# Moving a weight cast out of the down product's queue, and one gate into another PSUM bank, in an attention and bilinear-GLU kernel

## The chip, the cores and the metric

The kernel runs on one core of a Trainium2 chip. The metric is the device time of one execution in microseconds (us); differences under about 0.2% (4.6 us) cannot be told from no change. A profile is one execution: its rows give start times in us from the start of the span. PE is TensorE (PEld its weight loads), DVE is VectorE, ACT ScalarE, POOL GpSimd, and SP issues the DMAs.

## The reference

One pre-norm transformer layer on 2048 rows of 576 numbers, all in fp32: attention with 32 query heads of 18 and one shared key and value head, then a bilinear gated feed-forward part of width 4608 without a nonlinearity.

```python
def _A_ref(x, wq, wk, wv, wo):          # x: 1 x 2048 x 576, H = 32, Dh = 18
    q = (x @ wq).reshape(B, S, H, Dh).transpose(0, 2, 1, 3)
    k = x @ wk
    v = x @ wv
    scores = jnp.einsum("bhqd,bkd->bhqk", q, k) * (Dh ** -0.5)
    p = _softmax(scores, axis=-1)
    o = jnp.einsum("bhqk,bkd->bhqd", p, v)
    return o.transpose(0, 2, 1, 3).reshape(B, S, H * Dh) @ wo

def _B_ref(x, w_gate, w_up, w_down):
    g = jnp.einsum("bsd,df->bsf", x, w_gate)
    u = jnp.einsum("bsd,df->bsf", x, w_up)
    return jnp.einsum("bsf,fd->bsd", g * u, w_down)

h = x + _A_ref(_layernorm(x), wq, wk, wv, wo)
h2 = h + _B_ref(_layernorm(h), w_gate, w_up, w_down)
```

## The kernel before

The 2048 rows are worked on in four blocks of 512 (`NB`, `TB`). Each large fp32 product is made of three products of a rounded high part and a low part: a number is split into `hi` (a cast to the type fp32r) and `lo = x - f32(hi)`. The helper `split` issues both, the cast on an engine of the caller's choice (line L96 of the profile) and the subtraction on VectorE (L97).

The feed-forward part of blocks 0 to 2 is `ffn(b)`. It loops over 36 tiles of 128 hidden columns; tile `n_` is 36 b + f. For a tile TensorE runs 27 slots `j` (nine chunks of the input by three hi/lo combinations), in each slot one matmul for the gate (`pg`) and one for the up half (`pu`), line L1069. ScalarE copies the gate to `hf` (L1101), VectorE multiplies it by the up half (L1105). Two tiles make a pair; the down product of a pair (`down`, L1019) is issued at the end of the next even tile. It consists of 14 stages of three matmuls each (a seven-product scheme for 2 x 2 blocks), written out in the table `STAGES`, over three PSUM banks. After each stage the bank is added into the residual `h`: directly on VectorE (L1025, stages 0, 1, 3, 7, 9, 10, 12, 13), or by a copy to `tmp` on ScalarE (L1029) and an add on GpSimd (L1030; stages 2, 4, 5, 6, 8, 11). `tmp` has three buffers. Stages 9, 10, 12 and 13 begin a new sum in the banks of stages 6, 7, 9 and 10. The input of the down product is a split of `hf` and of sums `S` of its halves (`left`, `left_sums`, written to `room`).

Tiles are of two kinds. While attention work is left (`on`), its score matmuls and exponentials (L701, L702) and its value products (`acc`, L706) are laced into the gate/up slots; this holds for tiles 0 to 92. The last 15 tiles, 93 to 107, have none left and are called plain here. In plain tiles gate and up share the tile `gu` in PSUM, in the others each has a bank of its own: `ps_f` gives one of two banks in turn, `ps_m` and `ps_a` one each. `ps_a` is also the bank of the attention accumulator. At the end of an even tile the accumulator is closed (`flush(..., True)`): its last value products are issued, and VectorE saves it to `ob` (L719 or L748).

The order of the work on each engine is the order in which the code issues it (the schedule is manual); every engine works through its own queue, and so does the DMA queue of SP. The weights of a tile come in three steps: `load_w(n)` issues a DMA of 576 KB into `wr` (one buffer), and `split_w(n)` casts it on GpSimd into `ws` (two buffers) and subtracts on VectorE. The load of the next weights is issued behind the subtraction that frees `wr`. In plain tiles the split of the next tile's weights is issued at slot 9 of odd tiles, and in even tiles inside the down product, behind its stage 5.

When block 2 ends, block 3 is prepared on the side (`ahead`) and computed by `last_block` with another scheme (L1291 are its first matmuls). In tile 100 GpSimd runs the small chain of the reciprocal root for block 3's layer norm (L117 to L127).

Of the kernel before, what the change touches and what calls it, by code (L numbers as in the profile page):

```python
# [19 lines left out]
F32R = mybir.dt.float32r  # L20
I32 = mybir.dt.int32
AF = mybir.ActivationFunctionType
ALU = mybir.AluOpType
# [3 lines left out]
P = 128  # L27
# [30 lines left out]
class Block:  # L58
# [881 lines left out]
            r = self.wr[n] = self.wp.tile([P, 9, P], F32, tag="wr", bufs=1, name=f"wr{n}")  # L940
            self.sp.dma_start(r, self.wgu[n % NF])

    def split_w(self, n):
        if n < NF * (NB - 1):
            r = self.wr.pop(n)
            w = self.ws[n] = self.wp.tile([P, 2, 9, P], F32R, tag="ws", bufs=2, name=f"ws{n}")
            self.split(w[:, 0], w[:, 1], r, self.nc.gpsimd.tensor_copy)

    def load_wd(self, n):

# [91 lines left out]
    def ffn(self, b):  # L1042
        pe, act, dve = self.pe, self.act, self.dve
        X, hid, todo = self.X, [], None
        ahead = self.ahead()
        if b == 0:
            self.sums = self.weight_sums()
            next(self.sums)
        for f in range(NF):
            n_ = NF * b + f  # L1050
            k = f % 2
            w = self.ws.pop(n_)
            on = self.more(b + 2)
            self.cast_left = self.nc.gpsimd.tensor_copy if on else act.copy
            last = f == NF - 1 and b + 1 < NB
            end = b == NB - 2
            if on:
                pg = (self.ps_a if k and f > 1 and not last else self.ps_f)(f"pg{n_}")
                pu = (self.ps_f if k else self.ps_m)(f"pu{n_}")
            else:  # L1060
                gu = self.ps_s(f"gu{n_}")
                pg, pu = gu[:, 0], gu[:, 1]
            j = 0
            for c in range(9):
                for wk, xk in ((0, 0), (0, 1), (1, 0)):
                    if on and j in (PAIRS[2] if last else PAIRS[k]) and self.more(b + 2):
                        self.pair()
                    for o, ps in ((0, pg), (64, pu)):
                        pe.matmul(ps, w[o:o + 64, wk, c], X[o:o + 64, xk, c], start=(j == 0), stop=(j == 26))  # L1069
                    if j == (8 if on else 2) and todo and not plain(n_ - 2):  # L1070
                        self.left_sums()
                    if j == (3 if on else 9 if k else 27):
                        self.split_w(n_ + 1)
                    if j == (14 if on else 9 if k else 27):
                        self.load_w(n_ + 2)
                    if j == 5 and k:
                        self.left_first(n_ - 1, hid[0])
                    if j == 6 and not k:
                        self.split_wo()
                    if j == 12:  # L1080
                        self.run_aux(within=True, wo=False)
                    if 0 < f < NF - 1 and j in (8, 16, 24) and self.sums:
                        if next(self.sums, "end") == "end":
                            self.sums = None
                            self.load_wd(self.n_wd + 2)
                    if j == 6 and last and not end:
                        self.normal(b + 1)
                    if end and f == TURN - 1 and j == 12:
                        self.normed[NB - 1] = self.mv, self.rstd(self.mv[:, :, 1], "bl", self.nc.gpsimd)
                    if end and f in AHEAD and j in AHEAD[f]:  # L1090
                        for _ in range(AHEAD[f][j]):
                            next(ahead)
                    j += 1
            if todo and not on:
                for i, _ in enumerate(self.down(b, *todo)):
                    if i == 5:
                        self.split_w(n_ + 1)
                        self.load_w(n_ + 2)
                self.load_wd(self.n_wd + 7)
            hf = self.hh.tile([P, TB], F32, tag="hf", bufs=2, name=f"hf{n_}")  # L1100
            act.copy(hf, pg)  # L1101
            for _ in range(2 if on and not k else 0):
                if self.more(b + 2):
                    self.pair()
            dve.tensor_tensor(hf, pu, hf, ALU.mult)  # L1105
            hid.append(hf)
            if k:
                self.left(n_ - 1, hid)
                hid = []
            if end and f in TURNS:  # L1110
                for _ in range(TURNS[f]):
                    next(ahead)
            if not k or last:
                self.flush(len(self.pend), True)
            if todo and on:
                drain(self.down(b, *todo))
                self.load_wd(self.n_wd + 7)
            if f < NF - 1:
                self.run_aux(wo=k)
            todo = (f // 2,) if k else None  # L1120
        if end:
            del X, pg, pu, gu, w, ps, hf, self.X
            self.last_block(ahead, self.down(b, *todo))
            return
        both(self.spread(b + 1), self.down(b, *todo))
        self.load_wd(self.n_wd + 4)
        if b + 2 < NB:
            self.load_x(b + 2)
# [524 lines left out]
def both(a, b):  # L1653

    live = [a, b]
    while live:
        live = [x for x in live if next(x, drain) is not drain]


def plain(n):  # L1660

    return n % NF == NF - 2
# [6 lines left out]
def f32(ap):  # L1669
    return ap.bitcast(F32)  # L1670
# [20 lines left out]
def drain(gen):  # L1691
    for _ in gen:
        pass
# [85 lines left out]
```

## Time and profile before

| | us |
|---|---|
| median of 3 runs | 2297.33 (2295.97 to 2300.37) |
| profiled execution | 2295.53 |
| its span | 2293.7 |
| the plain tiles, 93 to 107, within it | 1785.5 to 1966.5 |
| VectorE's weight subtraction (L97), mean of 108 | 1.774 |
| GpSimd's weight cast (L96), mean of 108 | 1.193 |
| GpSimd's add into h (L1030), mean of 306 | 0.806 |

A row of a timeline names start, length, engine, line, operation, the tile written and the tiles read, shapes, a count (neighbouring instructions of one kind are merged) and, in brackets, how long the engine had been idle before and what ended that. A chain of waits is followed from the last instruction back: each piece is what the next one had to wait for.

### The profile page before, as it was taken

What the parts mean: (1) busy time and instruction counts of PE and PEld (TensorE: products, weight loads), DVE (VectorE), ACT (ScalarE), POOL (GpSimd) and SP (SyncE); (2) the same over time, 40 slices, a digit from 0 to 9 for tenths busy, and PEclk for the clock granted to TensorE, in tenths of its full rate; (3) what the DMA queues carried; (4) which work ended last, traced back from release to release, by engine and by line L of the source; (5) the groups of instructions that cost most, each with busy time, mean ns of one, the idle gap of its engine ahead of it and who ended that gap; (6) DMA issues with size and microseconds to landing.
All of it is one profiled execution on the core that took longest, in us unless ns stands there. A gap on an engine that the chain in (4) does not pass through costs nothing.

```text
span 2293.7 us, 45953 instructions
## 1 busy us (share of the span) xinstructions
PE 2239.2 (98%) x17972; PEld 1650.8 (72%) x17972; DVE 1380.1 (60%) x2234; ACT 1426.3 (62%) x1925; POOL 871.0 (38%) x956
## 2 busy tenths in 40 slices
PE   7999999999999999999999999999999888999999
PEld 5333345777777777777777787777777777899999
DVE  8555645555555566456555566545455666778876
ACT  7888877666666665666666666566666223555553
POOL 4445301444443444344443444342333342322222
PEclk9999999999999999999999999999999999999999
DMA  5879843555555554655554555653333344577775
GB/s 174 265 255 304 267 146 107 156 163 175 170 164 155 168 169 152 220 161 166 157 169 151 168 162 167 193 164 109 123 126 117 121 158 148 181 249 242 231 249 177
DMA packets 200433, 407.01 MB, mean 177 GB/s; under 512 B 22637, under 2 KB 54509, under 8 KB 200213
## 3 DMA queue, kind: packets, MB, share of 16 engines
q1 hardware_dynamic: 197621, 393.42, 53.8%
q0 software_dynamic: 2592, 10.62, 1.5%
q8 instruction: 143, 2.34, 0.4%
q14 instruction: 77, 0.63, 0.1%
HBM read 317.27 MB, written 74.55 MB: 171 GB/s over the span
## 4 chain that ended last, share of the span: by engine, by line
PE 82%; POOL 1%; DVE 1%; ACT 1%; DMA 1%; issue 1%; SPq 0%; ACTq 0%; POOLq 0%; DVEq 0%
PE pg L1069 16%; PE acc L706 15%; PE y L1019 12%; PE pu L1069 8%; PE s L701 8%; PE gs L1291 8%; PE gu L1069 4%; PE yq L1256 4%; PE yo L864 3%; PE gs L1298 1%; PE y L989 1%; POOL h L1030 1%; DVE ws L97 1%; ACT P L702 0%; DMA h<-in_x_dram 0%
## 5 line engine op out<-in xcount | busy, mean ns | idle before, releaser
L702 ACT ACTIVATE P<-s 128x1024 f32<-128x1024 f32 x1024 | 1009.9, 1028 | 222.7 <-PE s L701 141.6
L1069 PE MATMUL pg<-X,ws 64*128 64x512 f32 x2511 | 681.5, 389 | 4.5 <-ACT hf L1101 4.5
L1069 PE MATMUL pu<-X,ws 64*128 64x512 f32 x2511 | 681.2, 389 | 0.2
L1069 PEld LDWEIGHTS pg<-X,ws 64*128 64x128 f32 x2511 | 464.8, 185 | 60.2 <-issue 6.9
L1069 PEld LDWEIGHTS pu<-X,ws 64*128 64x128 f32 x2511 | 464.1, 185 | 25.7 <-ACT tmp L996 0.9
L706 PE MATMUL acc<-P,V 128*32 128x512 f32 x4096 | 480.0, 597 | 0.1
L701 PE MATMUL s<-q,kT 56*128 56x512 f32 x2048 | 430.9, 414 | 4.6 <-ACT P L702 3.5
L1030 POOL TENSOR_TENSOR h<-h,tmp 128x288 f32<-128x288 f32 x306 | 238.8, 806 | 406.2 <-ACT tmp L1029 391.4
L1029 ACT COPY tmp<-y 128x288 f32<-128x288 f32 x306 | 122.1, 399 | 380.5 <-PE y L1019 353.8
L1019 PEld LDWEIGHTS y<-wdo,room 128*128 128x128 f32 x2142 | 294.5, 191 | 67.5 <-issue 37.7
L1019 PE MATMUL y<-wdo,room 128*128 128x288 f32 x2142 | 309.8, 303 | 25.4 <-DVE h L1025 25.4
L701 PEld LDWEIGHTS s<-q,kT 56*128 56x128 f32 x2048 | 204.6, 184 | 167.2 <-ACT P L702 116.3
L706 PEld LDWEIGHTS acc<-P,V 128*32 128x32 f32 x4096 | 114.6, 109 | 255.1 <-issue 250.2
L97 DVE TENSOR_TENSOR ws<-wr,ws 128x1152 fp32r<-128x1152 f32 x108 | 191.6, 1774 | 119.3 <-POOL ws L96 117.8
L1025 DVE TENSOR_TENSOR h<-h,y 128x288 f32<-128x288 f32 x408 | 175.2, 452 | 121.0 <-PE y L1019 120.9
L1105 DVE TENSOR_TENSOR hf<-pu,hf 128x512 f32<-128x512 f32 x93 | 63.7, 685 | 224.9 <-ACT hf L1101 224.9
L96 POOL CAST room<-hf 128x256 fp32r<-128x256 f32 (+1 forms) x92 | 58.1, 632 | 320.1 <-DVE hf L1105 320.1
L96 POOL CAST ws<-wr 128x1152 fp32r<-128x1152 f32 x108 | 128.9, 1193 | 120.6 <-DMA wr<-in_wgu_dram 103.0
L1239 POOL TENSOR_TENSOR wsum<-wsum,wsum 128x512 f32<-128x512 f32 x72 | 144.8, 2011 | 44.8 <-DMA wsum<-in_wgs_dram 33.7
L1069 PE MATMUL gu<-X,ws 64*128 64x512 f32 x810 | 98.8, 401 | 0.0
L97 DVE TENSOR_TENSOR room<-hf,room 128x256 fp32r<-128x256 f32 (+1 forms) x108 | 94.9, 879 | 3.3 <-ACT room L96 1.9
L1069 PEld LDWEIGHTS gu<-X,ws 64*128 64x128 f32 x810 | 81.1, 193 | 15.9 <-issue 1.5
(268 smaller groups left out, 2756.5 us busy)
## 6 DMA issues: line engine op xcount, KB each, us to landing
wdo<-wd_dram SPq DMA_DIRECT2D x492, 288.0 KB
wr<-in_wgu_dram SPq DMA_DIRECT2D x108, 576.0 KB
wsum<-in_wgs_dram SPq DMA_DIRECT2D x108, 256.0 KB
wd_dram<-wd_room SPq DMA_DIRECT2D x20, 1008.0 KB
wsum_dram<-wsum SPq DMA_DIRECT2D x72, 256.0 KB
raw<-wsum_dram SPq DMA_DIRECT2D x72, 256.0 KB
q<-q_dram SPq DMA_DIRECT2D x64, 216.0 KB
raw<-in_wgs_dram SPq DMA_DIRECT2D x54, 256.0 KB
```

The source lines that it names most:

```text
L96: (copy or self.cast)(hi, src)
L97: self.dve.tensor_tensor(lo, src, f32(hi), ALU.subtract)
L701: self.pe.matmul(s_[:, i], self.kT[o:o + 56, t * P:(t + 1) * P], q[o:o + 56, pr], start=True, stop=True)
L702: self.act.activation(p_, s_, AF.Exp, scale=SCALE)
L706: self.pe.matmul(acc[32 * j:32 * j + 32, :], self.V[:, t, :], Ps[j // 2][:, j % 2, :], start=first, stop=last, skip_group_check=True)
L1019: pe.matmul(y[:, :HD], m[:, t * P:(t + 1) * P], k, start=(first and j == 0), stop=(j == 2), skip_group_check=True)
L1025: dve.tensor_tensor(hs, hs, y[:, :HD], ALU.add)
L1029: act.copy(z, y[:, :HD])
L1030: pool.tensor_tensor(hs, hs, z, ALU.add)
L1069: pe.matmul(ps, w[o:o + 64, wk, c], X[o:o + 64, xk, c], start=(j == 0), stop=(j == 26))
L1239: pool.tensor_tensor(to, x, y, op)
L1291: pe.matmul(bank[:, g * HT:(g + 1) * HT], W[:, wk, c, g], X[:, 2 * xk + c], start=(first and g == c == wk == xk == 0), stop=(c == 1 and wk ...
```

## The change

In the even plain tiles (94, 96, ... 106) the two halves of `split_w` are taken apart. The cast of the next tile's weights is issued at slot 3 of the tile's own gate/up matmuls. The subtraction and the load behind it are issued inside the down product, behind its stage 6 instead of 5; between these stages VectorE has nothing, so its order stays what it was. In the first odd tile of blocks 0 to 2 (tiles 1, 37 and 73) the gate's sum is put in the accumulator's bank, as it already is in later odd tiles.

```diff
-    def split_w(self, n):
+    def split_w(self, n, parts=(0, 1)):
         if n < NF * (NB - 1):
-            r = self.wr.pop(n)
-            w = self.ws[n] = self.wp.tile([P, 2, 9, P], F32R, tag="ws", bufs=2, name=f"ws{n}")
-            self.split(w[:, 0], w[:, 1], r, self.nc.gpsimd.tensor_copy)
+            for i in parts:
+                if i == 0:
+                    w = self.ws[n] = self.wp.tile([P, 2, 9, P], F32R, tag="ws", bufs=2, name=f"ws{n}")
+                    self.nc.gpsimd.tensor_copy(w[:, 0], self.wr[n])
+                else:
+                    w = self.ws[n]
+                    self.dve.tensor_tensor(w[:, 1], self.wr.pop(n), f32(w[:, 0]), ALU.subtract)
...
-                pg = (self.ps_a if k and f > 1 and not last else self.ps_f)(f"pg{n_}")
+                pg = (self.ps_a if k and not last else self.ps_f)(f"pg{n_}")
...
                     if j == (3 if on else 9 if k else 27):
                         self.split_w(n_ + 1)
+                    if j == 3 and not on and not k:
+                        self.split_w(n_ + 1, (0,))
...
                 for i, _ in enumerate(self.down(b, *todo)):
-                    if i == 5:
-                        self.split_w(n_ + 1)
+                    if i == 6:
+                        self.split_w(n_ + 1, (1,))
                         self.load_w(n_ + 2)
```

GpSimd's queue around tiles 97 to 100, before (`ws99` are the split weights of tile 99, `h2` is the residual of block 2, `vbl` belongs to block 3's layer norm; a count at the end stands for equal rows in succession):

```order
L96 CAST ws98_27700<-wr98_27589 128x1152
L1030 TENSOR_TENSOR h2_16941<-h2_16941,tmp_10403 128x288 x3
L96 CAST ws99_27852<-wr99_27703 128x1152
L1030 TENSOR_TENSOR h2_16941<-h2_16941,tmp_10403 128x288 x3
L96 CAST ws100_27932<-wr100_27855 128x1152
L117 TENSOR_SCALAR vbl_28009<-mvb3_27711 128x4
```

and now:

```order
L948 CAST ws98_27700<-wr98_27594 128x1152
L948 CAST ws99_27776<-wr99_27703 128x1152
L1034 TENSOR_TENSOR h2_16941<-h2_16941,tmp_10403 128x288 x6
L948 CAST ws100_27932<-wr100_27860 128x1152
L948 CAST ws101_27991<-wr101_27935 128x1152
L117 TENSOR_SCALAR vbl_28011<-mvb3_27711 128x4
```

The casts of the odd tiles' weights have moved ahead of all six adds into h of the down product, and that of tile 101 ahead of the layer norm's chain.

TensorE's queue at the start of tile 1 (the last value products of the accumulator, the scores of the next attention step, the first gate and up matmuls; in brackets the engines whose semaphores a row waits for, with the number of the semaphore), before:

```order
L706 MATMUL acc1_0_10516<-P1_0_15_1_10511,V_87 32x512 [waits Activation_49]
L706 MATMUL acc1_0_10516<-P1_0_15_1_10511,V_87 32x512
L701 MATMUL s1_1_0_0_10538<-q1_1_10104,kT_86 128x512 [waits PE_49]
L701 MATMUL s1_1_0_0_10538<-q1_1_10104,kT_86 128x512
L1069 MATMUL pg1_10536<-X0_10336,ws1_10427 128x512 [waits Pool_49]
L1069 MATMUL pu1_10537<-X0_10336,ws1_10427 128x512
```

and now:

```order
L706 MATMUL acc1_0_10516<-P1_0_15_1_10511,V_87 32x512 [waits Activation_49]
L706 MATMUL acc1_0_10516<-P1_0_15_1_10511,V_87 32x512
L701 MATMUL s1_1_0_0_10538<-q1_1_10104,kT_86 128x512 [waits PE_49]
L701 MATMUL s1_1_0_0_10538<-q1_1_10104,kT_86 128x512
L1073 MATMUL pg1_10536<-X0_10336,ws1_10427 128x512 [waits DVE_49,Pool_49]
L1073 MATMUL pu1_10537<-X0_10336,ws1_10427 128x512
```

Tile 1's gate now also waits for VectorE.

TensorE's queue from the end of tile 1 to the start of tile 2, before:

```order
L701 MATMUL s1_1_3_1_10648<-q1_1_10104,kT_86 128x512 [waits Activation_49]
L701 MATMUL s1_1_3_1_10648<-q1_1_10104,kT_86 128x512
L1069 MATMUL pg1_10536<-X0_10336,ws1_10427 128x512
L1069 MATMUL pu1_10537<-X0_10336,ws1_10427 128x512
L1069 MATMUL pg2_10664<-X0_10336,ws2_10551 128x512 [waits Activation_49,Pool_49]
L1069 MATMUL pu2_10665<-X0_10336,ws2_10551 128x512 [waits DVE_49]
```

and now:

```order
L701 MATMUL s1_1_3_1_10648<-q1_1_10104,kT_86 128x512 [waits Activation_49]
L701 MATMUL s1_1_3_1_10648<-q1_1_10104,kT_86 128x512
L1073 MATMUL pg1_10536<-X0_10336,ws1_10427 128x512
L1073 MATMUL pu1_10537<-X0_10336,ws1_10427 128x512
L1073 MATMUL pg2_10664<-X0_10336,ws2_10551 128x512 [waits Pool_49]
L1073 MATMUL pu2_10665<-X0_10336,ws2_10551 128x512
```

Tile 2's gate no longer waits for ScalarE, nor its up half for VectorE.

## The prediction

> **What bounds the kernel now.** I read the page first, then the list of what TensorE waited for, then the chain of waits in the stretch that this list points to, then the engines' timelines there. The page:
>
> ```profile
> span 2293.7 us, 45953 instructions
> PE 2239.2 (98%) x17972; PEld 1650.8 (72%) x17972; DVE 1380.1 (60%) x2234; ACT 1426.3 (62%) x1925; POOL 871.0 (38%) x956
> ```
>
> TensorE is busy for 98% of the span, so only its idle time, and busy time at a low clock, can be won. Two rows of its waits belong to the code that changes (waited for: us in total, times, longest):
>
> ```profile
> PE y L1019 <- DVE h L1025: 25.4, 7, 3.7
> ...
> PE pg L1069 <- ACT hf L1101: 4.5, 3, 1.5
> ```
>
> The first is the down product of the seven even plain tiles (94, 96, ... 106). The second is at the start of the third tile of blocks 0 to 2. The chain of waits through tile 98's down product:
>
> ```profile
> 1855.13 0.80 POOL h L1030
> 1855.93 1.10 POOL ws L96
> ...
> 1857.05 1.93 DVE ws L97
> ...
> 1858.98 0.38 DVE h L1025
> ...
> 1859.40 3.25 PE y L1019 x12
> ```
>
> Read upwards: stage 10 of the product starts its sum anew in the bank of stage 7, so it waits for VectorE's add of stage 7. That add is queued behind the weights' subtraction, the subtraction waits for GpSimd's cast, and the cast is queued behind three adds into h. TensorE's timeline (start, length; in brackets the idle time before):
>
> ```profile
> 1779.65 5.93 PE L1019 MATMUL y<-wdo,room 128*128 128x288 f32 x42
> 1785.51 12.54 PE L1069 MATMUL gu<-X,ws 64*128 64x512 f32 x108
> 1797.97 4.30 PE L1019 MATMUL y<-wdo,room 128*128 128x288 f32 x30
> ...
> 1851.53 4.28 PE L1019 MATMUL y<-wdo,room 128*128 128x288 f32 x30
> 1859.40 3.25 PE L1019 MATMUL y<-wdo,room 128*128 128x288 f32 x12 [3.60 <-DVE h L1025]
> 1862.57 12.62 PE L1069 MATMUL gu<-X,ws 64*128 64x512 f32 x108
> ...
> 1892.64 2.40 PE L1149 MATMUL txl<-C,xhl 128*128 128x128 f32 x20
> ...
> 1966.47 3.12 PE L1291 MATMUL gs<-XS,wrs 128*128 128x256 f32 x24
> ```
>
> The row at 1779.65 is a down product without a weight step in it: 5.86 us from its start to the next row's. Tile 98's takes 11.04. Its idle time is 3.60; the other 1.6 are in its last twelve matmuls, 3.25 us where 12/42 of 5.86 is 1.67. The granted clock says why (stretch, length, busy times; the number before the DMA share is the clock):
>
> ```profile
> 1851.50:1855.83 4.33, 4.30 (x32) 4.04 (x30) 1.30 (x3) 1.93 (x5) 2.27 (x3) 1.00 0.00 0
> 1859.40:1862.60 3.20, 3.20 (x14) 2.92 (x14) 1.22 (x3) 0.89 (x2) 1.59 (x2) 0.50 0.76 259
> 394.70:398.00 3.30, 3.22 (x28) 3.12 (x30) 3.07 (x6) 1.79 (x2) 0.86 (x1) 1.00 0.85 250
> ```
>
> After 3.60 us of idling TensorE runs at half clock for about 3 us; after the second kind of wait, 1.5 us before 394.78, it does not.
>
> **Part one, the plain tiles: what there is to win.** From 1785.51 to 1966.47 are 180.96 us. Clean, the work in it takes: 15 gate/up tiles at half of 12.46 (1785.51 to 1797.97), 93.5; seven down products at 5.86, 41.0; 40 output-projection matmuls at the pace of the row below, 5.4; 20 transposes, 2.4. Together 142.3, so 38.7 us are lost: 25.4 idle, the rest nearly all half clock.
>
> ```profile
> 1694.87 3.24 PE yo L864 x24
> ```
>
> **What of it stays.** Seven casts of 1.15 us leave the chain. The seven subtractions stay at the same place of VectorE's queue, behind the add of stage 3. The other engines' rows for tile 98:
>
> ```profile
> 1853.42 0.45 DVE L1025 TENSOR_TENSOR h<-h,y 128x288 f32<-128x288 f32 x1 [0.35 <-PE y L1019]
> 1857.05 1.93 DVE L97 TENSOR_TENSOR ws<-wr,ws 128x1152 fp32r<-128x1152 f32 x1 [3.17 <-POOL ws L96]
> ...
> 1853.55 2.38 POOL L1030 TENSOR_TENSOR h<-h,tmp 128x288 f32<-128x288 f32 x3 [13.30 <-ACT tmp L1029]
> 1855.87 1.14 POOL L96 CAST ws<-wr 128x1152 fp32r<-128x1152 f32 x1
> ...
> 1853.88 1.19 ACT L1029 COPY tmp<-y 128x288 f32<-128x288 f32 x3 [0.41 <-PE y L1019]
> 1855.50 0.40 ACT L1029 COPY tmp<-y 128x288 f32<-128x288 f32 x1 [0.42 <-PE y L1019]
> ```
>
> With its cast done, the subtraction can start at 1853.87, where GpSimd is in the first of its three adds (1853.55 to 1854.34). The two engines get in each other's way there:
>
> ```profile
> 1864.55 1.35 DVE L97 TENSOR_TENSOR ws<-wr,ws 128x1152 fp32r<-128x1152 f32 x1
> ...
> 386.51 1.52 DVE L97 TENSOR_TENSOR ws<-wr,ws 128x1152 fp32r<-128x1152 f32 x1
> 387.95 1.52 DVE L97 TENSOR_TENSOR room<-hf,room 128x256 fp32r<-128x256 f32 x1
> ...
> 386.78 2.41 POOL L1239 TENSOR_TENSOR wsum<-wsum,wsum 128x512 f32<-128x512 f32 x1
> ...
> 403.07 1.28 POOL L1239 TENSOR_TENSOR wsum<-wsum,wsum 128x512 f32<-128x512 f32 x1 [2.62 <-issue]
> ```
>
> Alone the subtraction takes 1.35; at 1857.05, just behind the start of the GpSimd add that follows the cast (1855.87 + 1.14; 2.38 / 3 = 0.79 long), it takes 1.93. At 386.78 a GpSimd sum that came behind a subtraction took 2.41 instead of 1.28, and VectorE's next small subtraction waited in turn. So they alternate. The Trainium skill, "SBUF — State Buffer" (Who interferes with whom), has this as a lock: a VectorE instruction with two SBUF inputs and a GpSimd one that reads SBUF exclude each other, and whichever issued first holds the port for its whole length. By that rule too the subtraction comes second in line, and the first rival below could not happen.
>
> I take: wait for the rest of the first add (0.47, of which about 0.14 hides, as at 1857.05, where 0.72 of overlap gave 0.58 of delay), then 1.35: done at 1855.55. The add of stage 7, 0.45, ends near 1855.95. TensorE is ready for stage 10 at 1851.53 + 4.30 = 1855.83: 0.2 us of waiting where 3.60 were. Late next is GpSimd: its second add waits for the subtraction and ends near 1856.2; ScalarE's fifth copy (1855.50) needs that add's buffer, ends near 1856.65 and frees the bank of stage 11, for which TensorE is ready at 1856.4: 0.3 us. So 0.5 us a down product, 3.5 us in all. Bounds: 0, if VectorE gets ahead of the first add, and 1.9 each, if it gets its turn after all three adds.
>
> **The cast's new place.** It waits at the head of GpSimd's queue for its weights. In tile 98 the load went out behind the subtraction that ended at 1858.98, and the rows here show when a cast could use it, 4.1 us later:
>
> ```profile
> 1863.11 1.15 POOL L96 CAST ws<-wr 128x1152 fp32r<-128x1152 f32 x1 [0.54 <-DMA wr<-in_wgu_dram]
> ...
> 1869.66 0.20 POOL L127 TENSOR_TENSOR ybl<-tbl,ybl 128x4 f32<-128x4 f32 x1
> ```
>
> The next load goes out at 1865.9 and lands near 1870.0; the even tile's third slot is near 1868.8 + 0.7, so the cast runs from 1870.0 to 1871.2, and the first add into h comes near 1877 (the product starts at 1862.57 + 12.46 = 1875.0, and tile 98's first add came 2.0 behind its product's start): 5.8 us of cover. Until then only the small reciprocal-root chain of block 3 (16 operations, ended 1869.66) is behind it, in tile 100: it now starts near 1871.2, takes 5.3 us or more, and may delay the adds by 0 to 1.5 us. The cast also holds up VectorE's sums S for 0 to 1.15 us; most down products have that much room, tile 94's (whose chain runs into the product) may lose 0.6. I book 1.5 us for these and 1 us for ScalarE's waits in one output projection, which stay. The step at SP is the same in both kernels: each load is still behind its subtraction, only earlier. Part one: 38.7 - 3.5 - 2.5 = 32.7 us won.
>
> **Part two, the first odd tiles (1, 37, 73).**
>
> ```profile
> 394.78 0.46 PE L1069 MATMUL pg<-X,ws 64*128 64x512 f32 x1 [1.51 <-ACT hf L1101]
> ...
> 394.05 0.58 ACT L1101 COPY hf<-pg 128x512 f32<-128x512 f32 x1
> ...
> 385.05 0.69 DVE L719 TENSOR_TENSOR ob<-ob,acc 128x512 f32<-128x512 f32 x1 [2.99 <-PE acc L706]
> ...
> 385.25 0.40 PE L1069 MATMUL pg<-X,ws 64*128 64x512 f32 x1
> ...
> 1480.94 0.69 DVE L719 TENSOR_TENSOR ob<-ob,acc 128x512 f32<-128x512 f32 x1 [2.99 <-PE acc L706]
> ...
> 1485.30 0.45 PE L1069 MATMUL pg<-X,ws 64*128 64x512 f32 x1
> ```
>
> Tile 2's gate takes the buffer of tile 1's gate and waits 1.51 us until ScalarE, late by its exponentials, has copied it. With tile 1's gate in the accumulator's bank that wait goes, three times: 4.5 us. In its place tile 1 waits for VectorE's save of the accumulator: it ends at 385.74 where the gate now starts at 385.25, so about 0.55 us. In block 2 an output projection stands between (save at 1480.94, gate only at 1485.30), nothing there. Net 4.5 - 2 x 0.55 = 3.4 (bounds 2.9 and 4.5).
>
> **Sum.** 36.1 us. The profiled execution took 2295.53 us (1.8 around its span), so 2259.4; the median of the runs shown is 1.8 higher, 2297.33, so 2261. A change under 0.2% (4.6 us) could not be told from none here.
>
> **Rivals.**
> 1. *The subtraction comes only after all three GpSimd adds* (1855.93 + 1.35 + 0.45 = 1857.7): TensorE idles 1.9 us a product instead of 0.5. At full clock afterwards 9.8 us less are won: 2271. With half clock, 1.6 more each: 2282. For it: GpSimd's adds are back to back. Against it: the alternation at 386. Whether 1.9 us cost the clock the rows leave open (1.51 did not, 3.60 did). The Trainium skill, "TensorE: Matmul & The Clock Gate" (What's actually happening), puts the fall to half rate after an idle window of about 3.4 us; by that rule it is 2271, not 2282, and the trace agrees as far as its two points go.
> 2. *Nothing is left over*: VectorE ahead of GpSimd's first add, no delays of S: 2256.
> 3. *Loads take it back*: the products follow each other in 12.46 + 5.86 = 18.3 us instead of 12.46 + 11.04 = 23.5, and the last two share the DMA queues with the last block's weights. If these two waited 4 to 5 us each: 2270.
> 4. *Slower: the cast blocks GpSimd's queue.* If the weights landed later than 5.8 us behind the time above, every add into h, and TensorE behind it, would wait. It decides against the change from a landing 5.8 + 5.5 (38.7 / 7) us later, some 15 us after issue instead of 4.1; at 20 us it gives 2297 + 7 x 4.5 = 2329, less 3. Nothing in the rows comes near it.
> 5. *No change*: VectorE's queue stays the bound by some other wait of the same size; no row shows one.
>
> **How the numbers follow.** Forecast (2256 to 2266) 0.62; rival 1 at full clock 0.14, at half clock 0.05; rival 2 0.08; rival 3 0.06; rival 4 0.03; rival 5 0.02. The range 2254 to 2277 takes in the forecast, rivals 2 and 3, and rival 1 at full clock; it leaves out the rest. Faster 0.95, same 0.02, slower 0.03.
>
> **What would show it.** TensorE's 42 matmuls of an even plain down product in one piece of 6.2 to 6.5 us; the wait of y for h under 4 us in total; a granted clock near 1.00 behind it; the subtraction starting within 0.1 us of the third VectorE add and taking 1.7; the casts under the gate/up matmuls. The wait of pg for hf gone and one for the accumulator's save there, twice, near 0.5. I am wrong if the subtraction still starts two microseconds or more behind the third add, if GpSimd shows a long wait for wr, or if the last block's first matmuls wait for weights.

## The result and the profile after

The changed kernel takes 2263.55 us (median of 4 runs, 2262.34 to 2263.72) against 2296.82 for the kernel before in the same comparison: a ratio of 0.9851, with a 95% interval from 0.9834 to 0.9868, or 33.3 us faster. The forecast was 2261.0. The profiled execution took 2262.34 us, its span is 2260.6. The line numbers have moved: the gate/up matmuls are now L1073, the down product L1023, its adds on VectorE L1029, the copies on ScalarE L1033, the adds on GpSimd L1034; the weights' cast is L948, their subtraction L951.

The page of the kernel after:

```profile
span 2260.6 us, 45951 instructions
PE 2229.9 (99%) x17972; PEld 1653.0 (73%) x17972; DVE 1381.2 (61%) x2234; ACT 1426.6 (63%) x1925; POOL 882.5 (39%) x956
```

TensorE has the same 17972 matmuls and 9.3 us less busy time, since the half clock is gone; the rest of the 33.1 us of span is idle time. Its waits (us in total, times, longest):

```profile
PE s L701 <- ACT P L702: 4.5, 13, 1.0
...
PE y L1023 <- ACT tmp L1033: 2.2, 1, 2.2
...
PE pg L1073 <- DVE ob L719: 0.9, 2, 0.5
PE y L1023 <- DVE h L1029: 0.9, 5, 0.2
```

The wait of the down product for VectorE fell from 25.4 us to 0.9. The wait of the gate's bank for ScalarE (4.5 us, three times) is not in the list any more; the two waits for the accumulator's save that were forecast at 0.55 each are 0.47 each. One row is new: 2.2 us at one single place, for ScalarE's copy. The first row, the scores' wait for exponentials, stood at 3.5 us before (12 times, 0.4 at most); one of 1.0 us has come to it, in block 1 (in the six kernels below that also have the new bank the longest is 0.4 to 1.4 us). TensorE's timeline in the plain tiles:

```profile
1781.84 12.55 PE L1073 MATMUL gu<-X,ws 64*128 64x512 f32 x108
...
1839.88 4.27 PE L1023 MATMUL y<-wdo,room 128*128 128x288 f32 x30
1844.34 2.17 PE L1023 MATMUL y<-wdo,room 128*128 128x288 f32 x12 [0.19 <-DVE h L1029]
1846.44 12.54 PE L1073 MATMUL gu<-X,ws 64*128 64x512 f32 x108
1858.91 3.88 PE L1023 MATMUL y<-wdo,room 128*128 128x288 f32 x27
1864.96 2.28 PE L1023 MATMUL y<-wdo,room 128*128 128x288 f32 x15 [2.17 <-ACT tmp L1033]
1867.18 6.42 PE L1073 MATMUL gu<-X,ws 64*128 64x512 f32 x54
...
1933.26 3.12 PE L1297 MATMUL gs<-XS,wrs 128*128 128x256 f32 x24
```

Tile 98's down product takes 6.56 us from its start to the next gate/up row (1839.88 to 1846.44), where it took 11.04. Tile 100's takes 8.27 (1858.91 to 1867.18), where it took 10.87. The plain stretch takes 151.42 us (1781.84 to 1933.26) where it took 180.96: 29.5 us won. It begins 3.67 us earlier, which is part two and about half a microsecond of drift that is there before block 0's feed-forward tiles. Behind it nothing is given back: 2293.7 - 1966.47 = 327.2 us before, 2260.6 - 1933.26 = 327.3 after. The granted clock behind the 0.19 us wait of tile 98 (stretch, length, busy time of TensorE, its weight loads, VectorE, ScalarE and GpSimd with counts, clock, DMA share, GB/s):

```profile
1844.34:1847.30 2.96, 2.89 (x20) 2.38 (x22) 1.91 (x5) 1.29 (x3) 2.96 (x5) 1.00 0.75 256
```

It is 1.00 here, and also behind the longer wait of tile 100. VectorE and GpSimd in the same product:

```profile
1841.77 0.45 DVE L1029 TENSOR_TENSOR h<-h,y 128x288 f32<-128x288 f32 x1 [0.35 <-PE y L1023]
1842.14 1.78 DVE L951 TENSOR_TENSOR ws<-wr,ws 128x1152 fp32r<-128x1152 f32 x1
1843.84 0.81 DVE L1029 TENSOR_TENSOR h<-h,y 128x288 f32<-128x288 f32 x2
...
1834.07 1.15 POOL L948 CAST ws<-wr 128x1152 fp32r<-128x1152 f32 x1 [5.45 <-DMA wr<-in_wgu_dram]
1841.90 5.74 POOL L1034 TENSOR_TENSOR h<-h,tmp 128x288 f32<-128x288 f32 x6 [6.68 <-ACT tmp L1033]
```

The cast starts 7.8 us ahead of the first add into h. The subtraction starts right behind the add of stage 3 and takes 1.78 us, the 0.43 above its 1.35 alone being the wait for the rest of GpSimd's first add. What is left over is in the chain of waits through this product:

```profile
1841.90 0.80 POOL h L1034
...
1842.71 1.88 POOL h L1034
...
1844.61 0.41 ACT tmp L1033
...
1845.07 1.46 PE y L1023 x9
```

GpSimd's first add takes 0.80. Its second, behind the subtraction, takes 1.88; that holds up ScalarE's fifth copy, and this copy the matmuls of stage 11.

### The profile page after: what moved, and what is told of

Same layout as the page of the kernel before. It is cut to its first block, busy times and chain, and to the rows that moved or that the text cites. A ratio compares the mean times of both kernels' runs of the same rounds, so it can differ in the third digit from the quotient of the medians.

```text
span 2260.6 us, 45951 instructions
## 1 busy us (share of the span) xinstructions
PE 2229.9 (99%) x17972; PEld 1653.0 (73%) x17972; DVE 1381.2 (61%) x2234; ACT 1426.6 (63%) x1925; POOL 882.5 (39%) x956
## 4 chain that ended last, share of the span: by engine, by line
PE 81%; DMA 2%; POOL 1%; DVE 1%; ACT 1%; issue 1%; SPq 0%; ACTq 0%; POOLq 0%; DVEq 0%
PE pg L1073 17%; PE acc L706 15%; PE y L1023 12%; PE s L701 8%; PE gs L1297 8%; PE pu L1073 8%; PE yq L1262 4%; PE gu L1073 3%; PE yo L864 3%; PE gs L1304 2%; POOL h L1034 1%; PE y L993 1%; DMA out_dram<-h 1%; DMA wr<-in_wgu_dram 1%; DMA h<-in_x_dram 0%
## 5 line engine op out<-in xcount | busy, mean ns | idle before, releaser
L1073 PE MATMUL pg<-X,ws 64*128 64x512 f32 x2511 | 680.6, 389 | 0.9 <-DVE ob L719 0.9
L1073 PE MATMUL pu<-X,ws 64*128 64x512 f32 x2511 | 680.5, 389 | 0.2
L1073 PEld LDWEIGHTS pg<-X,ws 64*128 64x128 f32 x2511 | 465.0, 185 | 52.1 <-issue 2.7
L1073 PEld LDWEIGHTS pu<-X,ws 64*128 64x128 f32 x2511 | 464.2, 185 | 22.3 <-ACT tmp L1000 0.9
L1034 POOL TENSOR_TENSOR h<-h,tmp 128x288 f32<-128x288 f32 x306 | 244.5, 829 | 335.8 <-ACT tmp L1033 333.5
L1033 ACT COPY tmp<-y 128x288 f32<-128x288 f32 x306 | 122.3, 400 | 356.0 <-PE y L1023 314.0
L1023 PEld LDWEIGHTS y<-wdo,room 128*128 128x128 f32 x2142 | 290.5, 188 | 47.3 <-issue 38.5
L1023 PE MATMUL y<-wdo,room 128*128 128x288 f32 x2142 | 306.8, 301 | 3.5 <-ACT tmp L1033 2.2
L951 DVE TENSOR_TENSOR ws<-wr,ws 128x1152 fp32r<-128x1152 f32 x108 | 189.9, 1759 | 100.0 <-POOL ws L948 100.0
L1029 DVE TENSOR_TENSOR h<-h,y 128x288 f32<-128x288 f32 x408 | 175.3, 452 | 118.0 <-PE y L1023 117.9
L948 POOL CAST ws<-wr 128x1152 fp32r<-128x1152 f32 x108 | 131.2, 1215 | 153.1 <-DMA wr<-in_wgu_dram 141.5
L1245 POOL TENSOR_TENSOR wsum<-wsum,wsum 128x512 f32<-128x512 f32 x72 | 145.2, 2017 | 45.4 <-DMA wsum<-in_wgs_dram 36.1
L1073 PE MATMUL gu<-X,ws 64*128 64x512 f32 x810 | 94.5, 389 | 0.0
L1073 PEld LDWEIGHTS gu<-X,ws 64*128 64x128 f32 x810 | 80.3, 184 | 11.9 <-issue 1.5
```

The source lines that it names most:

```text
L948: self.nc.gpsimd.tensor_copy(w[:, 0], self.wr[n])
L951: self.dve.tensor_tensor(w[:, 1], self.wr.pop(n), f32(w[:, 0]), ALU.subtract)
L1023: pe.matmul(y[:, :HD], m[:, t * P:(t + 1) * P], k, start=(first and j == 0), stop=(j == 2), skip_group_check=True)
L1029: dve.tensor_tensor(hs, hs, y[:, :HD], ALU.add)
L1033: act.copy(z, y[:, :HD])
L1034: pool.tensor_tensor(hs, hs, z, ALU.add)
```

## The experiments

**The two parts, one at a time.** Two theories stood open: that the parts are independent, or that part of the gain of one is only there with the other. The first kernel has the moved cast without the change of bank, the second the change of bank alone.

```diff
-                pg = (self.ps_a if k and not last else self.ps_f)(f"pg{n_}")      # after
+                pg = (self.ps_a if k and f > 1 and not last else self.ps_f)(f"pg{n_}")
```

> Part one alone: the cast at the third slot and the subtraction within the down product, the first odd tile's gate where it was before. If the two parts are independent and the plain tiles carry the gain, this wins the 29.5 us by which the stretch of tiles 93 to 107 became shorter (180.96 to 151.42): about 2267, and three waits of 1.51 us of pg for hf are back. If part of the gain came from the two parts together, it lies above 2270.

```diff
-                pg = (self.ps_a if k and f > 1 and not last else self.ps_f)(f"pg{n_}")      # before
+                pg = (self.ps_a if k and not last else self.ps_f)(f"pg{n_}")
```

> Part two alone. Independent parts: three waits of 1.51 us go, two of 0.47 us for the accumulator's save come, and tile 38's scores wait once for an exponential (0.97 us in the changed kernel): 2.6 to 3.4 us won, 2293.5 to 2294.2. If ScalarE, which is late by its exponentials there, only moves the wait, 0 to 1 us are won: 2296 to 2297.

The cast alone: 2267.44 us against 2297.13, ratio 0.9872 (0.9857 to 0.9887), 29.7 us. The bank alone: 2293.04 against the same 2297.13, ratio 0.9982 (0.9973 to 0.9991), 4.1 us. Together 33.8, and the whole change gave 33.3: within the intervals (some 2 to 4 us to either side) the gains add up, so neither part needs the other. TensorE's waits with the cast alone, then with the bank alone:

```profile
PE pg L1073 <- ACT hf L1107: 4.5, 3, 1.5
```

```profile
PE y L1019 <- DVE h L1025: 25.5, 7, 3.7
...
PE pg L1069 <- DVE ob L719: 0.9, 2, 0.5
```

Each part takes away its own wait and leaves the other's. The new wait of 2.2 us for ScalarE's copy is there with the cast alone and not with the bank alone.

**The cast behind one and behind two of GpSimd's adds.** In the kernel before it is behind three, after behind none. This doses the wait that stage 10 had, and it asks from which wait on the clock is lost. Both kernels are the one after with the cast back in the down product; for two adds the number 2 is a 4. Both also have the gate's new bank, so for three adds the time to set beside theirs is that of the bank alone (2293.0), not that of the kernel before.

```diff
-                    if j == 3 and not on and not k:
-                        self.split_w(n_ + 1, (0,))
...
                 for i, _ in enumerate(self.down(b, *todo)):
+                    if i == 2:
+                        self.split_w(n_ + 1, (0,))
                     if i == 6:
```

> As the changed kernel, but the cast of the even plain tiles goes into the down product behind its stage 2, so one of GpSimd's adds stands ahead of it (three before the change, none after). By the chain, in tile 98's times of before: add until 1854.34, cast until 1855.5, subtraction with one add against it 1.93, add 0.45: TensorE waits 2.0 us in each of the seven products. If the clock is kept after 2.0 us of idling (the rule of an idle window of about 3.4 us), the product takes 7.9 to 8.1 us instead of 6.6: about 2273.5, and the granted clock behind the wait is near 1.0. If 2.0 us are enough to lose the clock, 1.6 us more each: about 2285, with a clock near 0.5 behind the wait.

> As before, with the cast behind stage 4: two adds ahead of it. The chain gives a wait of 2.8 us in each product. Clock kept: 8.7 us a product, about 2279. Clock lost: 10.3 us a product, about 2290. A mixture, with the half clock behind some of the seven waits only, would speak for a window that runs on its own and that a wait of 2.8 us fills sometimes.

Behind one add: 2273.2 us, ratio 0.9893 (0.9878 to 0.9908). Behind two: 2283.91, ratio 0.9943 (0.9928 to 0.9959). The row of the wait, with one add ahead and with two:

```profile
PE y L1023 <- DVE h L1029: 14.1, 7, 2.0
```

```profile
PE y L1023 <- DVE h L1029: 20.1, 7, 2.9
```

Stage 10 waits 0.2, 2.0, 2.9 and 3.6 us for a cast behind none, one, two and three adds, with one to three in all seven tiles alike, with none in five of them (tiles 94 and 100 have other delays): the chain of the prediction, with the time in step (2263.6, 2273.2, 2283.9 and 2293.0). The clock is not in step. With one add ahead, the last twelve matmuls of tiles 98 and 102, which waited equally long:

```profile
1850.18 1.86 PE L1023 MATMUL y<-wdo,room 128*128 128x288 f32 x12 [2.01 <-DVE h L1029]
...
1893.87 3.22 PE L1023 MATMUL y<-wdo,room 128*128 128x288 f32 x12 [2.00 <-DVE h L1029]
```

The same wait leaves the clock alone in one tile and halves it in the other. In the profiled executions it was lost behind two of the seven waits of 2.0 us (tiles 94 and 102), three of the seven of 2.9 (94, 98 and 104), and six of the seven of 3.6 in the kernel before (the exception is tile 96): the mixture that the second expectation named.

What separates the waits is where they lie. The traces record the times at which the granted clock changes. In all nine traces they lie on a grid of 3.413 us (within 4 ns), and in the plain tiles a half clock lasts one piece of that grid, for tile 94 in the kernel before and with the bank alone two (6.83 us). The pieces around the waits of tiles 98 and 102 with one add ahead (start and end, length, TensorE's busy time first; the clock stands before the DMA share), and the piece in which tile 96's wait begins in the kernel before:

```profile
1846.15:1849.57 3.42, 2.02 (x15) 1.78 (x14) 1.82 (x2) 1.59 (x4) 3.42 (x4) 1.00 0.00 0
1849.57:1852.98 3.41, 2.80 (x20) 2.50 (x22) 2.68 (x7) 0.89 (x2) 3.15 (x4) 1.00 0.60 205
1890.53:1893.94 3.41, 1.41 (x11) 1.17 (x10) 2.42 (x3) 1.00 (x3) 3.41 (x3) 1.00 0.00 0
1893.94:1897.35 3.41, 3.41 (x14) 3.13 (x16) 1.38 (x4) 0.89 (x2) 2.47 (x4) 0.50 0.82 260
```

```profile
1828.64:1832.06 3.42, 1.57 (x12) 1.33 (x10) 0.57 (x1) 1.22 (x4) 3.34 (x5) 1.00 0.00 0
```

The wait of tile 102 lies in one piece, in which TensorE idles 2.0 us, and the next piece runs at half clock. The wait of tile 98 is cut by the end of a piece into 1.4 and 0.6 us, and the clock stays. Tile 96's, of 3.63 us, is cut nearly in the middle. Over all nine traces (without the first 20 and the last few us of each), half clock followed each of the 16 full-clock pieces in which TensorE idled 1.96 us or more, one of the four with 1.82 to 1.86 us, and two of all the others. These two, at 50.7 and 50.8 us with one add ahead and in the kernel of the whole split below, follow pieces with 0.45 us of idling and stay unexplained.

**The layer norm's chain ahead of the cast.** In tile 100 ScalarE's copy waits for GpSimd, whose queue holds the cast of tile 101's weights and behind it block 3's small chain. In the kernel after:

```profile
1855.99 1.42 POOL L948 CAST ws<-wr 128x1152 fp32r<-128x1152 f32 x1 [6.83 <-DMA wr<-in_wgu_dram]
1857.50 1.07 POOL L117 TENSOR_SCALAR vbl<-mvb 128x4 f32<-128x4 f32 x1
...
1861.41 1.17 POOL L127 TENSOR_TENSOR ybl<-tbl,ybl 128x4 f32<-128x4 f32 x1
...
1863.54 0.20 POOL L127 TENSOR_TENSOR ybl<-tbl,ybl 128x4 f32<-128x4 f32 x1
1863.69 4.61 POOL L1034 TENSOR_TENSOR h<-h,tmp 128x288 f32<-128x288 f32 x6
...
1864.51 0.40 ACT L1033 COPY tmp<-y 128x288 f32<-128x288 f32 x1 [2.44 <-POOL h L1034]
...
1849.36 1.34 DVE L951 TENSOR_TENSOR ws<-wr,ws 128x1152 fp32r<-128x1152 f32 x1
...
1856.92 1.57 DVE L97 TENSOR_TENSOR room<-S,room 128x1024 fp32r<-128x1024 f32 x1 [0.52 <-ACT room L96]
...
1861.18 1.35 DVE L951 TENSOR_TENSOR ws<-wr,ws 128x1152 fp32r<-128x1152 f32 x1
```

The cast waits for its weights until 1855.99, the chain runs until 1863.74, and the adds into h come only then, 4.8 us behind the product's start where tile 98's came 2.0 behind it. In this kernel the chain is issued at slot 2 instead of 12, ahead of the cast.

```diff
-                    if end and f == TURN - 1 and j == 12:
+                    if end and f == TURN - 1 and j == 2:
```

> As the changed kernel, but GpSimd's chain for block 3's layer norm in tile 100 is issued at slot 2 instead of 12, so ahead of the cast at slot 3. If the wait of 2.17 us in tile 100's product comes from the chain that the cast pushed back, it goes: product 6.6 us, 2.0 to 2.3 us won (with half clock behind it a little more): about 2261.3. If it comes from something else in tile 100, nothing is won: 2263.5.

It took 2260.55 us against 2296.77, ratio 0.9842 (0.9828 to 0.9855); by the medians, which come from two comparisons, 3.0 us less than the kernel after, by the profiled spans 1.9. Tile 100's down product:

```profile
1858.71 4.31 PE L1023 MATMUL y<-wdo,room 128*128 128x288 f32 x30
1863.17 2.17 PE L1023 MATMUL y<-wdo,room 128*128 128x288 f32 x12 [0.15 <-DVE h L1029]
1865.28 6.41 PE L1073 MATMUL gu<-X,ws 64*128 64x512 f32 x54
```

6.57 us instead of 8.27, like the other tiles': the chain behind the cast was the cause of the new wait.

**The whole split ahead of the product.** If the residue of each product is the subtraction between the adds of stages 3 and 7, it goes when the subtraction stands at slot 3 too. A rival has it that the residue comes from the product itself, from ScalarE's copies and the three buffers. In tiles where VectorE's work runs into the product, the subtraction ahead of it may cost something again.

```diff
                     if j == 3 and not on and not k:
-                        self.split_w(n_ + 1, (0,))
+                        self.split_w(n_ + 1)
+                        self.load_w(n_ + 2)
...
-                for i, _ in enumerate(self.down(b, *todo)):
-                    if i == 6:
-                        self.split_w(n_ + 1, (1,))
-                        self.load_w(n_ + 2)
+                drain(self.down(b, *todo))
```

> As the changed kernel, but the subtraction and the load behind it are issued at the third slot as well, ahead of the down product. If the 0.7 us that five of the seven products still take above 5.86 (0.18 of waiting for VectorE at stage 10, some 0.3 for ScalarE's copy at stage 11) come from the subtraction between the stages and its quarrel with GpSimd's adds, these products fall to 5.9 us: 3.5 us won; in tiles 94 and 96, where VectorE's chain runs into the product, 1.3 and 0.4 us may be lost again: 2261 to 2262. If they come from the product itself (the copies by ScalarE and the three buffers), nothing is won: 2263.5 or, with the losses, 2265.

2259.69 us against 2296.77, ratio 0.9840 (0.9827 to 0.9854). TensorE's rows for tiles 94, 98 and 104:

```profile
1797.16 4.69 PE L1023 MATMUL y<-wdo,room 128*128 128x288 f32 x33 [1.23 <-DVE h L1029]
...
1840.24 5.91 PE L1023 MATMUL y<-wdo,room 128*128 128x288 f32 x42
...
1900.96 4.70 PE L1023 MATMUL y<-wdo,room 128*128 128x288 f32 x33 [1.03 <-DVE h L1029]
```

The products of tiles 98, 102 and 106 run in one piece and take 5.84, 5.85 and 5.89 us, the clean product's time, so the residue was the subtraction, and the rival is out. The losses came too, in tile 94 as expected and in tile 104, where none was expected. In tiles 94 and 104 VectorE has other work up to the product's start (the split of an output projection's weights, sums for block 3); with the subtraction in that row the adds of stages 0 and 1 come late, and TensorE waits 1.23 and 1.03 us. That the time is below the 2261 to 2262 expected is largely tile 100's doing: its product takes 6.57 us (1858.55 to 1865.12) instead of 8.27, since its weights land earlier and GpSimd's cast and chain are done 2.1 us sooner (1861.66 instead of 1863.74).

**Both, from tile 98 on.** The chain first, and from tile 98 on the whole split at slot 3; tiles 94 and 96 stay as after.

```diff
-                        self.split_w(n_ + 1, (0,))
+                        self.split_w(n_ + 1, (0, 1) if f >= 26 else (0,))
+                        if f >= 26:
+                            self.load_w(n_ + 2)
...
-                    if i == 6:
+                    if i == 6 and f < 26:
```

(with slot 2 for the chain as above)

> Chain first as in the run before, and cast, subtraction and load at the third slot from tile 98 on (tiles 94 and 96 as in the changed kernel). If both residues are what the last two expectations say, 2.2 + 5 x 0.65 = 5.4 us under the changed kernel: about 2258, the fastest so far. If the subtraction ahead of the product only moves the delay to VectorE's first adds, 2261.

2259.07 us against 2296.77, ratio 0.9834 (0.9821 to 0.9848). Tiles 98, 100 and 104:

```profile
1839.64 5.91 PE L1023 MATMUL y<-wdo,room 128*128 128x288 f32 x42
1857.94 6.26 PE L1023 MATMUL y<-wdo,room 128*128 128x288 f32 x42
...
1899.97 4.70 PE L1023 MATMUL y<-wdo,room 128*128 128x288 f32 x33 [1.03 <-DVE h L1029]
```

This is the fastest of the kernels; its plain stretch takes 147.72 us, 3.7 less than after. But its interval overlaps that of the change (0.9834 to 0.9868), and beside the two experiments before it nothing was won that a comparison can tell. Tile 104 still loses the 1.03 us; a version that leaves that one as after was not run.

## Why the prediction was right, and where it was off

- **The chain.** Shown by the four positions of the cast: behind none, one, two and three adds stage 10 waits 0.2, 2.0, 2.9 and 3.6 us. The second and the third add in front cost 0.9 and 0.7 us of wait, about the length of an add; the first costs 1.8, since with it the cast comes into the chain.
- **The first rival** (the subtraction gets its turn only behind all three adds) is out: the subtraction ran behind the first add, in 1.78 us, forecast 1.68. The rule on the shared port, "SBUF — State Buffer" (Who interferes with whom) in the Trainium skill, has the two exclude each other, and the trace agrees in both directions: GpSimd's second add took 1.88 us behind the subtraction. That the subtraction comes ahead of the second add does not follow from that rule alone, as the prediction has it; the trace shows it.
- **The residue** was forecast at 0.2 for stage 10 and 0.3 for stage 11, and is 0.2 and about 0.5 (the last twelve matmuls 2.17 at full clock where 12/42 of a clean product are 1.67): 0.7 a product instead of 0.5. The mechanism was the one named, ScalarE's fifth copy behind GpSimd's second add; it came at 1844.61, 0.46 us behind the end of the 30 matmuls (1839.88 + 4.27), forecast 0.37. Over seven products 1.4 us. So a product takes 6.56 us in two pieces, where the prediction had 6.2 to 6.5 in one.
- **Tile 100** went beyond its bound. The delay of the layer norm's chain was seen, but bounded at 1.5 us and booked, with tile 94, at 1.5. Its wait is 2.17, and the product takes 2.4 more than clean. Two of the step's numbers were low: the weights were taken as landed 4.1 us behind the end of the subtraction, the cast here came 5.3 behind it (1849.36 + 1.34 to 1855.99; 3.9 in tile 98, 5.1 and 5.7 in tiles 104 and 106); and the chain took 6.2 us, not the 5.3 that stood as the least, because its first operation (0.37 in the kernel before) took 1.07 during VectorE's split of the sums (1856.92 to 1858.49), and a 0.20 us operation took 1.17 during the weights' subtraction (1861.18 to 1862.53). With the chain ahead of the cast the term goes to nothing. What was booked for tiles 94 and 100 together nearly held all the same: above the residue of 0.7 they lost 0.2 and 1.7.
- **The output projections** in the stretch take 3.87 (1801.12 to 1804.99) and 3.47 us where 40 matmuls at the clean pace are 5.4: 1.9 us, with 1 booked. Their rows:

```profile
1801.12 1.38 PE L864 MATMUL yo<-wos,room 128*128 128x288 f32 x9
...
1804.99 12.54 PE L1073 MATMUL gu<-X,ws 64*128 64x512 f32 x108
...
1823.94 1.24 PE L864 MATMUL yo<-wos,room 128*128 128x288 f32 x6
...
1827.41 12.53 PE L1073 MATMUL gu<-X,ws 64*128 64x512 f32 x108
```

- **Part one** was to win 32.7 us and won 29.5 in the stretch, 29.7 by itself. Of the 3.2 us between, the residue makes 1.4, the projections 0.9 and tiles 94 and 100 0.4; some 0.5 stays open. **Part two** was put at 3.4 and gave 4.1 (2.1 to 6.2 by its interval, so 3.4 is not excluded). Its two new waits have the size forecast, 0.47 where 0.55 stood. The scores' longer wait for exponentials was not in its sum; it is 1.0 us in the trace of the kernel after and not there in that of the whole split, so it is not sure that the change brings it. The sum, 36.1 against 33.3, is off by about the difference of these.
- **The loads** (the third rival) cost nothing that shows: the last block's first matmuls start without a wait, and the 327 us behind the stretch are the same. One sign that the prediction named for being wrong is there all the same: GpSimd waits long for `wr`, 5.45 us ahead of the cast in tile 98 and 6.83 in tile 100, since the cast now stands at the head of its queue before its weights have landed. It costs nothing where the first add comes later still, as in tile 98 (6.68 us behind the cast); in tile 100 it is part of the delay above.
- **The clock.** "After 3.60 us of idling TensorE runs at half clock" is true of six of seven waits, not of all. The prediction left open whether 1.9 us would cost the clock and weighed the rule of the Trainium skill, "TensorE: Matmul & The Clock Gate" (What's actually happening), of an idle window of about 3.4 us, by which it would not. The measurement decides against it as a threshold: waits of 2.0 us halved the clock in two tiles of seven. The grid of the traces has about that length (3.413 us), but a piece of it need not be idle throughout: 1.96 us in it were enough each time. For the result the clock hardly mattered: no wait of 0.2 us lost it. That the one of 2.17 us in tile 100 did not is luck in the profiled execution: the end of a piece, at 1864.54, cuts it into 1.75 and 0.42 us.

## What to carry to other kernels

An in-order queue passes on the wait of its first instruction to everything behind it: when one engine's work is late by the length of some other engine's instructions, look for a step that could have been issued earlier, and count the instructions in front of it. Before a cast that waits for a DMA is moved forward, look at what is queued behind it until its data can be there, small chains included; the delay comes out at the next buffer that they feed. A step between two stages of a product is best placed where its engine is idle in that very tile, which the trace tells tile by tile: what gained 0.7 us in each of three tiles lost 0.5 and 0.7 in two others.

## What the runs showed of the hardware

The half clock behind a wait depends on the wait's place as well as on its length. It came behind none of the waits of 0.2 us, two of seven of 2.0, three of seven of 2.9 and six of seven of 3.6, and equal waits (2.00 and 2.01 us) gave 0.50 and 1.00. In the nine traces the granted clock changes on a grid of 3.413 us only. A piece of the grid in which TensorE idled 1.96 us or more was followed by half clock each time (16 of 16), pieces with less than 1.82 us by none in the plain tiles. This is read from the records; no run moved a wait along the grid on purpose, and the two early falls behind pieces with 0.45 us of idling do not fit it.

VectorE and GpSimd hold each other up in both directions: the subtraction of 1.35 us took 1.78 behind a GpSimd add, the next GpSimd add of 0.80 took 1.88 behind the subtraction, and in tile 100 a GpSimd operation of 0.20 us took 1.17. In tile 98 the engine that waited got its turn before the next instruction in the other's queue.
